# A decode step on one Trainium2 core: PV in four column tiles of N=128, one PSUM group and one scaling per batch, all batches in one loop

## The chip, the core and the metric

The kernel runs on one NeuronCore of a Trainium2 chip. The core has five engines that run on their own and meet at semaphores: TensorE (PE in the profile; its weight loads are PEld), VectorE (DVE), ScalarE (ACT), GpSimd (POOL) and SyncE (SP), which here does nothing but issue DMAs. SBUF and PSUM have 128 partitions[...]. The metric is device microseconds of one execution. Before the change the median of five runs is 193.3 us (193.22 to 193.56).

## The reference, cut to what matters

One decode token for each of 8 batches: attention over the last 2048 positions of a cache of 8192, with 32 query heads on 8 KV heads of 128, then an output projection and an MLP.

```python
W = min(4096, max(256, Sk // 4))                       # 2048
rep = Hq // Hkv                                        # 4
x = A_x
q = (layernorm(x) @ wq).reshape(B, 1, 32, 128).transpose(0, 2, 1, 3)
k = jnp.repeat(k_cache[:, :, Sk - W:, :], rep, axis=1)
v = jnp.repeat(v_cache[:, :, Sk - W:, :], rep, axis=1)
p = softmax(einsum("bhqd,bhkd->bhqk", q, k) * Dh ** -0.5)
o = einsum("bhqk,bhkd->bhqd", p, v)
h = x + o.transpose(0, 2, 1, 3).reshape(B, 1, 4096) @ wo
x = layernorm(h)
h2 = gelu(layernorm(x) @ w3) @ w4                      # hs is zero for one token
out = h + x + h2
```

The inputs are bf16. B_w1 and B_w2 have no influence on the result for a sequence of one token, and the kernel doesn't load them.

## The kernel before, in words

**Tiles.** K and V of a batch are each two tiles of four KV heads (`gq` 0 and 1), 2048 KB per tile: 16 K tiles and 16 V tiles. A tile lies in one of ten SBUF slots (`slots`, 16 KB per partition): partition p holds 64 positions of one of its four heads. The last two slots hold `wq` first and `wo` at the end; `w3` and `w4` take K slots at the end.

**Loads.** SP issues everything on one queue in the order of the list `order` (L229): wq, four K tiles, two V tiles at once; then, alternating, a K tile four ahead and a V tile, each after a wait until the slot's earlier user is done (`free_slot`, L253: `sem_Thi` for K, `sem_PV` for V); then the last V tiles, wo in four pieces, w3 in two, w4 in three.

**One K tile** is worked on in four quarters (t = 0 to 3 for the first tile of a batch, 4 to 7 for the second). `pe_T` (L456) turns a quarter into 16 transposes of 128x128 into one of two PSUM tiles `kT_ps`. ScalarE takes out the first half (`act_Elo`, L494), VectorE the second (`dve_Ehi`, L498), into `kT_sb`. `pe_QK` (L502) then multiplies: four matmuls of N=512 in four column tiles of 32, one for each KV head, all 64 of a batch into one bank of `S_ps`. A quarter can be transposed once the quarter two before it has been taken out.

**Softmax** of a batch: VectorE finds the maximum (`dve_max`), ScalarE makes the exponentials in two halves (`act_exp`), TensorE transposes them (`pe_P`, L480, 16 transposes, into the same `kT_ps`), VectorE multiplies by a 0/1 mask that keeps each head's own rows (`dve_pT`, L572), which gives the weights `pT_sb` for PV. The sums take a fp32 matmul (`pe_LB`), a reciprocal and a product (`dve_rL`).

**PV** of a V tile (`pe_PV`, L581) is 16 matmuls with 64 columns of weights and N=512: the moving side is four position quarters times 128, so each of the four query positions in PSUM has its result in another quarter of the bank. VectorE gathers them with one scaled copy and three scaled adds (`dve_O1`, L602), TensorE adds partitions with `hsel` (`pe_oT`), VectorE copies to `o_all` (`dve_oT`). At the very end `pe_place` and the copies behind it spread `o_all` over 128 partitions as `opl`, for the projection (`pe_proj`).

**Order.** Batch 0 is written out; batches 1 to 7 are a loop on TensorE (`pe_block`, L663, `pe_main`, L701). A pass with batch i transposes and scores batch i, makes P of batch i-1 and PV of batch i-2, so that PV and other work lie between steps that wait. The parts with PV stand in branches that the first pass leaves out (`If_ne`, L667). VectorE and ScalarE have no loop: their instructions are listed in order (L716 and following). Where TensorE waits in the loop, it uses `need`: an instruction that waits for a semaphore and subtracts what it waited for.

**Tail.** After the loop come PV of the last two batches, placement, the projection (128 matmuls, each group of wo pieces behind its wait), statistics, w3 (56 matmuls), gelu, and w4 (56 matmuls of N=128 in four column tiles, behind waits for three pieces), then the store.

Of the kernel before, what the change touches and what calls it, by code (L numbers as in the profile page):

```python
# [11 lines left out]
B = 8  # L12
# [19 lines left out]
NS = 10  # L32
# [4 lines left out]
def bass_sequential_preLN__sliding_block_cached__mixer_s_mlp__decode_kernel(  # L37
# [24 lines left out]
    with es:  # L62
# [30 lines left out]
        P_sb = sb([128, CC * 128], dt.bfloat16, "P_sb")  # L93
        pT_sb = sb([128, 2, CC, 64], dt.bfloat16, "pT_sb")
        maskT = sb([128, CC // 2 * GL, 32], dt.bfloat16, "maskT")
        sel = sb([128, GL], dt.float32, "sel")
        headc = sb([128, NT * R], dt.float32, "headc")
        lspread = sb([128, 128], dt.float32, "lspread")
        par_sel = sb([128, 2, GL * R], dt.float32, "par_sel")
        hsel = sb([128, GL * R], dt.float32, "hsel")  # L100
        gq_of = sb([128, 2], dt.float32, "gq_of")
        qi_of = sb([128, NT], dt.float32, "qi_of")
        mrl = sb([128, 2, 2, NT], dt.float32, "mrl")
        o_sum = sb([128, 2, DH], dt.float32, "o_sum")
        mtile = sb([128, 3, 32], dt.float32, "mtile")
        mrow = sb([128, 3, 32], dt.float32, "mrow")
        lcol = sb([128, 2, 2], dt.float32, "lcol")
        lsum = sb([128, 1], dt.float32, "lsum")
        lsel = sb([128, 2], dt.float32, "lsel")
        rL = sb([128, 2, 2], dt.float32, "rL")  # L110
        iota_f = sb([128, 128], dt.float32, "iota_f")
        selp = sb([GL * R, NT, 4 * GL * R], dt.bfloat16, "selp")
        o_all = sb([GL * R, 2, B, DH], dt.bfloat16, "o_all")
# [28 lines left out]
        pv_ps = [misc, b6]  # L142
        LB = S_ps[:, 1, 0:2]
        OT = slice(0, DH)
        H3 = slice(384, 384 + FC * B)

        sem_slot = [S(f"sem_slot{i}") for i in range(NS)]
# [20 lines left out]
        sem_lsel = S("sem_lsel")  # L168
        sem_LB = S("sem_LB")
        sem_qc = S("sem_qc")  # L170
        sem_PV = S("sem_PV")
        sem_O1 = S("sem_O1")
        sem_oTm = S("sem_oTm")
        sem_oT = S("sem_oT")
        sem_oTA = S("sem_oTA")
        sem_pl = S("sem_pl")
# [31 lines left out]
        POOL_ZERO = 3  # L208

        def pool_prog(e):  # L210
            e.memset(eps_t[:, 0:1], EPS)
            e.memset(eps_t[:, 1:2], EPS * EPS / (1.0 + EPS))
            e.memset(zrow_b[:], 0.0)
            e.memset(scratch[:], 1.0).then_inc(sem_pool, 1)
            e.iota(iota_f[:], [[1, 128]], base=0, channel_multiplier=-1,
                   allow_small_or_imprecise_dtypes=True).then_inc(sem_pool, 1)
            e.memset(mean_w[:], 1.0 / D)
            e.memset(qcur[:], 0.0)
            e.memset(mtile[:], 0.0)
            e.memset(mrow[:], 0.0)  # L220
            e.memset(selp[:], 0.0).then_inc(sem_pool, 1)
# [6 lines left out]
        early = NTILE - 2  # L228
        order = [("k", t) for t in range(4)] + [("v", 0), ("v", 1), ("k", 4), ("v", early), ("k", 5)]  # L229
        for t in range(2, NTILE - 4):  # L230
            order += [("v", t), ("k", t + 4)]
        order += [("v", t) for t in range(NTILE - 4, NTILE) if t != early]
        order += [("wo", 0), ("wo", 1), ("w3", 0), ("w4", 0)]
        place = {("wo", 0): NS - 2, ("wo", 1): NS - 1, ("w3", 0): 0, ("w4", 0): 1}
        for t in range(NTILE):
            place["k", t] = 4 + t if t < 2 else t % 2
            place["v", t] = 4 + t - (NTILE - 4) if t >= NTILE - 4 else 2 + t % 2
        use = {}
        for key in order:
            use[key] = 1 + sum(place[k] == place[key] for k in use)  # L240
        for t in (-2, -1):
            place["v", t] = 4 + t
            use["v", t] = 0
# [6 lines left out]
        def sp_prog(e):  # L250
            e.dma_start(wq_sb, A_wq.rearrange("(p k) n -> p (k n)", k=KC)).then_inc(sem_wq, 16)

            def free_slot(kind, t):  # L253
                if kind == "k" and t >= 4:
                    e.wait_ge(sem_Thi, NT * (t - 1))
                elif kind == "v" and NTILE - 4 <= t < NTILE - 2:
                    e.wait_ge(sem_Thi, NT * (t - (NTILE - 4) + 1))
                elif kind == "v" and 2 <= t < NTILE - 4:
                    e.wait_ge(sem_PV, t - 1)
                elif kind == "wo":  # L260
                    e.wait_ge(sem_peP, PEP_Q2)
                elif kind in ("w3", "w4"):
                    e.wait_ge(sem_Thi, NITEM if kind == "w4" else NITEM - NT)

            for kind, t in order:
                free_slot(kind, t)
                slot = place[kind, t]
                dst = slots[:, slot, :]
                if kind in "kv":
                    b, gq = divmod(t, 2)  # L270
                    cache = A_k_cache if kind == "k" else A_v_cache
                    src = cache[b, GL * gq:GL * (gq + 1), W0:SK, :].rearrange("g (p c) d -> p g (c d)", c=C)
                    e.dma_start(dst, src).then_inc(sem_slot[slot], 16)
                elif kind == "wo":
# [11 lines left out]
                else:  # L286
                    w4_rows = B_w4.rearrange("(c p j) n -> p c (j n)", p=128, j=2)
# [20 lines left out]
        def dve_ident(e):  # L308
# [5 lines left out]
            with nc.allow_low_precision("sums of one 1 and zeros"):  # L314
                ins = e.tensor_reduce(sel[:, 0:GL], ident_f[:, :].rearrange("p (a g) -> p g a", g=GL), AX.X, ALU.add)
            chain(e, ins, "dve_self", dve_self)
            ins = e.tensor_copy(maskT[:, :, :].rearrange("p (c g) x -> p c g x", g=GL),
                                bass.AP(tensor=sel[:, :].tensor, offset=0, ap=[[GL, 128], [0, CC // 2], [1, GL], [0, 32]]))
            chain(e, ins, "dve_self", dve_self)
            with nc.allow_low_precision("sums of one 1 and zeros"):  # L320
                e.tensor_reduce(headc[:, :].rearrange("p (g r) -> p g r", r=R),
                                ident_f[:, :].rearrange("p (g x r) -> p g r x", g=GL, r=R), AX.X, ALU.add)
                e.tensor_reduce(par_sel[:, :, :].rearrange("p a (g r) -> p a g r", r=R),
                                ident_f[:, :].rearrange("p (a g q r) -> p a g r q", a=2, g=GL, r=R), AX.X, ALU.add)
                e.tensor_reduce(gq_of[:, :], ident_f[:, :].rearrange("p (g a x) -> p a g x", g=GL, a=2), AX.XY, ALU.add)
                ins = e.tensor_reduce(qi_of[:, :], ident_f[:, :].rearrange("p (a q r) -> p q a r", q=NT, r=R), AX.XY, ALU.add)
            chain(e, ins, "dve_self", dve_self)
            hc = bass.AP(tensor=headc[:, :].tensor, offset=0, ap=[[NT * R, 128], [R, GL], [0, NT], [1, R]])
            for a in range(2):
                e.tensor_scalar(lspread[:, 64 * a:64 * (a + 1)].rearrange("p (g q r) -> p g q r", g=GL, r=R),  # L330
                                hc, 0.25, None, ALU.mult)
            e.wait_ge(sem_pool, POOL_ZERO)
            for q in range(NT):
                e.tensor_copy(selp[:, q, :].rearrange("p (m q) -> p q m", q=NT)[:, q, :], ident_f[0:GL * R, 0:GL * R])
# [622 lines left out]
```

## Time and profile before

| | |
|---|---|
| median of five runs | 193.3 us (193.22 to 193.56) |
| the profiled execution | 193.35 us; its span, first to last instruction, 191.6 us |
| TensorE busy, weight loads busy | 145.1 us (76%), 98.4 us (51%) |
| VectorE, ScalarE, GpSimd busy | 105.5 us (55%), 90.4 us (47%), 1.9 us (1%) |
| moved by DMA | 79.31 MB, mean 414 GB/s over the span |
| transposes of K (L473) | 1024, 67.8 us busy |
| evictions of K, ScalarE (L496) and VectorE (L500) | 64 each, 1028 and 688 ns |
| QK (L516), PV (L595) | 256 matmuls in 22.5 us, 256 in 31.8 us |
| VectorE gathering PV (L608, L611) | 64 instructions, 22.3 us |
| mean granted TensorE clock | 0.968 |

How to read it: busy time is a union, so engines that work side by side each count in full, and the share says nothing on who waits for whom. In the slices of the page each digit is the busy share in tenths of one fortieth of the span, 4.8 us. A timeline row gives the start, the time, the engine, the line, the operation with what it writes and reads, and the number of instructions run together; in brackets stands how long the engine was idle before and who ended that. "DMA share" of a window is the mean busy share of the 16 DMA engines. The chain of waits is followed back from the last instruction to what released each step.

### The profile page before, as it was taken

Reading aid. Unit: us, or ns where it says so; the run is one execution under the profiler, and the core shown is the slowest. Engines: PE = TensorE matmul, PEld = TensorE weight load, DVE = VectorE, ACT = ScalarE, POOL = GpSimd, SP = SyncE. Lnnn points to the kernel's source line nnn. Section 1 sums busy time; section 2 is a strip of 40 time slices with the busy share of each in tenths; the row PEclk is TensorE's granted clock in tenths of the full one; section 3 lists DMA queues with packets and bytes.
Section 4 is the critical chain, followed back from the end, with each engine's and each line's share of the span. In section 5 each row is a group of like instructions: output and inputs, shape, how many; then the busy total and the mean of one; then the engine's idle time right before and its main releaser. Section 6 shows DMA issues by size and latency. Waiting matters only on the chain. (4 is left out here: it accounts for less than half of the span.)

```text
span 191.6 us, 4850 instructions
## 1 busy us (share of the span) xinstructions
PE 145.1 (76%) x2028; PEld 98.4 (51%) x2028; DVE 105.5 (55%) x287; ACT 90.4 (47%) x113; POOL 1.9 (1%) x14
## 2 busy tenths in 40 slices
PE   2027998797698769886988698958896888776854
PEld 0003976573656455645564557454655465343742
DVE  6401757564647474747474747565665657585141
ACT  3301676862746275526553664347344835406041
POOL 4000000000000000000000000000000000000000
PEclk9999999999999999999999999999999999999755
DMA  6999999999999999999999999999999999999991
GB/s 221 438 421 434 424 424 434 426 434 424 434 424 431 428 438 431 434 431 434 419 431 431 434 431 433 431 434 434 424 424 434 431 434 434 431 438 393 417 403 48
DMA packets 6857, 79.31 MB, mean 414 GB/s; under 512 B 688, under 2 KB 704, under 8 KB 2368
## 3 DMA queue, kind: packets, MB, share of 16 engines
q1 hardware_dynamic: 6832, 79.18, 97.4%
q8 instruction: 6, 0.10, 0.2%
q10 hardware_dynamic: 16, 0.01, 0.0%
q14 instruction: 3, 0.02, 0.0%
HBM read 79.18 MB, written 0.01 MB: 413 GB/s over the span
## 5 line engine op out<-in xcount | busy, mean ns | idle before, releaser
L496 ACT ACTIVATE kT_sb<-kT_ps 128x1024 bf16<-128x1024 bf16 x64 | 64.7, 1028 | 67.3 <-PE kT_ps L473 66.9
L473 PE MATMUL kT_ps<-perm_b,slots 128*128 128x128 bf16 x1024 | 67.8, 222 | 23.7 <-PEq L454 23.5
L473 PEld LDWEIGHTS kT_ps<-perm_b,slots 128*128 128x128 bf16 x1024 | 60.0, 100 | 34.6 <-issue 34.5
L500 DVE COPY kT_sb<-kT_ps 128x1024 bf16<-128x1024 bf16 x64 | 43.5, 688 | 26.2 <-PE kT_ps L473 26.1
L516 PE MATMUL S_ps<-kT_sb,qcur 128*32 128x512 bf16 x256 | 22.5, 387 | 0.8 <-PEq L454 0.8
L546 ACT ACTIVATE P_sb<-S_ps,mtile 128x1024 bf16<-128x1024 f32 x16 | 17.8, 1115 | 2.6 <-DVE mtile L537 2.5
L595 PE MATMUL b<-slots,pT_sb 128*64 128x512 bf16 x128 | 16.5, 384 | 1.2 <-PEq L454 1.2
L577 DVE TENSOR_TENSOR pT_sb<-kT_ps,maskT 128x1024 bf16<-128x1024 bf16 x16 | 10.5, 686 | 10.7 <-PE kT_ps L489 10.7
L595 PE MATMUL misc<-slots,pT_sb 128*64 128x512 bf16 x128 | 15.3, 382 | 0.6 <-PEq L454 0.6
L526 DVE TENSOR_REDUCE mtile<-S_ps 128x1 f32<-128x512 f32 x8 | 5.5, 692 | 13.6 <-PE S_ps L516 13.6
L595 PEld LDWEIGHTS misc<-slots,pT_sb 128*64 128x64 bf16 x128 | 6.7, 109 | 8.4 <-issue 3.6
L595 PEld LDWEIGHTS b<-slots,pT_sb 128*64 128x64 bf16 x128 | 6.2, 109 | 9.2 <-issue 5.7
L516 PEld LDWEIGHTS S_ps<-kT_sb,qcur 128*32 128x32 bf16 x256 | 5.3, 93 | 8.3 <-issue 4.2
L489 PEld LDWEIGHTS kT_ps<-ident_b,P_sb 128*128 128x128 bf16 x128 | 7.2, 98 | 4.1 <-issue 4.1
L489 PE MATMUL kT_ps<-ident_b,P_sb 128*128 128x128 bf16 x128 | 8.7, 219 | 0.6 <-PEq L454 0.6
L611 DVE SCALAR_TENSOR_TENSOR o_sum<-b,mrl,o_sum 128x128 f32<-128x128 f32 x24 | 8.4, 351 | 0.8
L611 DVE SCALAR_TENSOR_TENSOR o_sum<-misc,mrl,o_sum 128x128 f32<-128x128 f32 x24 | 8.4, 351 | 0.8
L395 PE MATMUL S_ps<-slots,xlnT 128*8 128x512 bf16 x32 | 3.6, 626 | 5.7 <-DMA slots<-in_A_wq_dram 5.7
L626 DVE CAST o_all<-misc 16x128 bf16<-16x128 f32 x7 | 1.9, 279 | 7.0 <-PE misc L620 7.0
L412 DVE TENSOR_SCALAR q_sb<-S_ps 128x512 bf16<-128x512 f32 x1 | 0.7, 691 | 9.1 <-PE S_ps L395 9.1
L395 PEld LDWEIGHTS S_ps<-slots,xlnT 128*8 128x8 bf16 x32 | 1.0, 117 | 7.5 <-issue 7.5
L657 ACT ACTIVATE opl<-kT_ps 128x224 bf16<-128x224 f32 x1 | 1.2, 1181 | 6.6 <-PE kT_ps L649 6.6
(104 smaller groups left out, 82.3 us busy)
## 6 DMA issues: line engine op xcount, KB each, us to landing
slots<-in_A_k_cache_dram SPq DMA_DIRECT2D x16, 2048.0 KB, 14.2
slots<-in_A_v_cache_dram SPq DMA_DIRECT2D x16, 2048.0 KB, 16.6
slots<-in_A_wq_dram SPq DMA_DIRECT2D x1, 4096.0 KB, 12.3
slots<-in_A_wo_dram SPq DMA_DIRECT2D x1, 2048.0 KB, 30.7
slots<-in_B_w_dram SPq DMA_DIRECT2D x2, 896.0 KB, 32.0
slots<-in_A_wo_dram SPq DMA_DIRECT2D x1, 1024.0 KB, 32.5
slots<-in_A_wo_dram SPq DMA_DIRECT2D x2, 512.0 KB, 33.7
slots<-in_B_w_dram SPq DMA_DIRECT2D x1, 1024.0 KB, 25.7
```

Source lines behind the costliest of these rows:

```text
L395: ins = e.matmul(S_ps[32 * j:32 * j + B, k, :], xlnT[:, kc * B:(kc + 1) * B], wq_v[:, kc, n0:n0 + 512], start=(kc == 0), stop=(kc == KC - ...
L473: ins = e.matmul(kT_ps[t % 2][:, c * 128:(c + 1) * 128], src[:, c * 128:(c + 1) * 128], perm_b[:, :], is_transpose=True)
L489: ins = e.matmul(kT_ps[half][:, c * 128:(c + 1) * 128], P_sb[:, half * W // 2 + c * 128:half * W // 2 + (c + 1) * 128], ident_b[:, :], is_ ...
L496: e.activation(kT_sb[:, i % NKT, 0:W // 2], kT_ps[i % 2][:, 0:W // 2], ACT.Copy).then_inc(sem_Elo, 1)
L500: e.tensor_copy(kT_sb[:, i % NKT, W // 2:W], kT_ps[i % 2][:, W // 2:W]).then_inc(sem_Ehi, 1)
L516: ins = e.matmul(S_ps[32 * gl:32 * (gl + 1), 0, :], qcur[:, GL * gq + gl, o:o + 32], kv[:, gl, :, :], start=(t == 0), stop=(t == 2 * NT - ...
L526: ins = e.tensor_reduce(mtile[:, 2, 0:1], S_ps[:, 0, :], AX.X, ALU.max)
L546: e.activation(P_sb[:, half * W // 2:(half + 1) * W // 2].rearrange("r (k g) -> r k g", g=GL), s_rep, ACT.Exp, bias=mtile[:, j, 0:1], scal ...
L577: e.tensor_tensor(pT_sb[:, :, half * hc:(half + 1) * hc, :].rearrange("p a c (g x) -> p (c g) a x", g=GL), kT_ps[half][:, 0:W // 2].rearra ...
L595: ins = e.matmul(pv_ps[gq][64 * a:64 * (a + 1), :].rearrange("p (q d) -> p q d", d=DH), pT_sb[:, gq, cc, :], vq[:, cc, :, :], start=(cc < ...
L611: ins = e.scalar_tensor_tensor(o_sum[:, gq, :], pv_ps[gq][:, q * DH:(q + 1) * DH], w[:, q:q + 1], o_sum[:, gq, :], ALU.mult, ALU.add)
L626: e.tensor_copy(o_all[:, gq, b, :], pv_ps[gq][0:GL * R, OT]).then_inc(sem_oT, 1)
```

## The change

- **PV** takes one V row of 128 per matmul: 64 matmuls of N=128 per V tile, with 32 columns of weights, in four column tiles of 32, one for each quarter q of the positions. Both V tiles of a batch add into one PSUM group (`pv_ps`, 128x128): the weights of a tile are 32 columns of a row of 48 in `pT_sb` whose other half is zero, so that heads of the one tile add nothing to the other.
- **Scaling**: one VectorE multiply by `rL` per batch (`dve_O1`) takes the place of two times four. The sums come straight from the two columns `lsum` that the exponentials leave, by two fp32 matmuls (`pe_LB`); the additions and products around them go.
- **Placement**: per batch four fp32 matmuls with `selw` (`pe_OP`) add the partitions and spread the result, and ScalarE copies it to `opl` (`act_OP`). `hsel`, `o_all`, `pe_oT`, `dve_oT`, `pe_place` and their copies go.
- **Loop**: all eight batches run in one loop on TensorE. A pass does the first four transposes, P and sums of the batch before, QK and the other transposes, the last QK, then PV and placement of the batch before, in a branch that the first pass leaves out. PV is one batch late, not two. The q transposes stand before the loop and so before the first K transposes. The loop's head is put at the start of an instruction block.
- **Loads**: nine slots. K tiles alternate between two slots, V tiles between two, the last batch's V tiles and w3 have slots of their own. SP's order is K0, K1, the last batch's first V tile, K2, V0, K3, V1, then per batch two K and two V tiles. K tile t waits until K tile t-2 is transposed; V tiles wait for the half of PV that used their slot.
- GpSimd clears `selw`, `lsum`, `P_sb` and `pT_sb` at the start; the constants of VectorE change with the layout.

```diff
-NS = 10
+NS = 9
-        pv_ps = [misc, b6]
-        LB = S_ps[:, 1, 0:2]
+        pv_ps = misc[:, 0:DH]
+        LB = S_ps[:, 1, 0:1]
...
+        order = [("k", 0), ("k", 1), ("vl", 0), ("k", 2), ("v", 0), ("k", 3), ("v", 1)]
+        for b in range(1, NB - 1):
+            order += [("k", 2 * b + 2), ("k", 2 * b + 3), ("v", 2 * b), ("v", 2 * b + 1)]
+        order += [("vl", 1), ("wo", 0), ("wo", 1), ("w3", 0), ("w4", 0)]
...
+                    if kind == "k" and b:
+                        e.wait_ge(sem_Thi, NT * (t - 1))
+                    if kind == "v" and b:
+                        e.wait_ge(sem_PV[gq], b)
...
+        def pe_P(e, i, half):
+            need(e, sem_exp, 2 * i + half + 1)
+            n = min(2 * NT * i + 3 + half, 2 * NT * NB)
+            need(e, sem_Elo, n)
+            need(e, sem_Ehi, n)
...
+        def pe_LB(e):
+            if e is not None:
+                for half in range(2):
+                    ins = e.matmul(LB, lspread[:, :, :].rearrange("p q h -> p (q h)"), lsum[:, half:half + 1],
+                                   start=(half == 0), stop=(half == 1))
+                ins.then_inc(sem_LB, 1)
...
+        def pe_PV(e, slot, gq, cs=range(CT)):
+            for c in cs:
+                for q in range(NT):
+                    k = q * CT + c
+                    ins = e.matmul(pv_ps[32 * q:32 * (q + 1), :], pT_sb[:, c, q, 16 * gq:16 * gq + 32],
+                                   slots[:, slot, k * DH:(k + 1) * DH], start=(gq == 0 and c == 0),
+                                   stop=(gq == 1 and c == CT - 1), tile_position=(0, 32 * q), skip_group_check=True)
+            if c == CT - 1:
+                ins.then_inc(sem_PV[gq], 1)
+
+        def dve_O1(e, b):
+            e.wait_ge(dve_self, cnt["dve_self"])
+            e.wait_ge(sem_PV[1], b + 1)
+            e.tensor_scalar(o_sum[:, :], pv_ps, rL[:, :], None, ALU.mult).then_inc(sem_O1, 1)
...
+        def pe_OP(e, b):
+            need(e, sem_O1, b + 1)
+            if e is None:
+                return
+            for q in range(4):
+                ins = e.matmul(op_ps(b), selw[:, q, :], o_sum[:, NJ * q:NJ * (q + 1)], start=(q == 0), stop=(q == 3))
+            ins.then_inc(sem_OP, 1)
...
+        def pe_block(e, i, later=None):
+            p = 2 * NT * i
+            for t in range(NT):
+                pe_T(e, i, t)
+            pe_P(e, i, 0)
+            pe_P(e, i, 1)
+            pe_LB(e)
+            pe_QK(e, p)
+            pe_QK(e, p + 1)
+            for t in range(NT, 2 * NT):
+                pe_T(e, i, t)
+                pe_QK(e, p + t - 2)
+            pe_QK(e, p + 6)
+            pe_QK(e, p + 7)
+            if i == 0:
+                return
+            with nullcontext() if e is None else e.If_ne(later, 0):
+                log.append("later")
+                for gq in range(2):
+                    need(e, sem_v[gq], 16 * i)
+                    if e is not None:
+                        pe_PV(e, 2 + gq, gq)
+                pe_OP(e, i - 1)
...
+            with nc.Fori(0, NB, engines=(mybir.EngineType.PE,), head_slot={mybir.EngineType.PE: 0}):
+                pe_block(e, 1, later_on)
+                e.reg_mov(later_on, 1)
...
+        def pe_last(e):
+            pe_P(e, NB, 0)
+            pe_P(e, NB, 1)
+            pe_LB(e)
+            e.wait_ge(sem_vl[0], 16)
+            for half in range(2):
+                need(e, sem_pT, 2 * NB + 1 + half)
+                pe_PV(e, 4, 0, range(half * CT // 2, (half + 1) * CT // 2))
+            e.wait_ge(sem_vl[1], 16)
+            pe_PV(e, 5, 1)
+            pe_OP(e, NB - 1)
```

On ScalarE a batch is now its eight evictions, the two exponentials, and the copy of the placement of the batch before; on VectorE the eight evictions with the two mask products and the reciprocal of the batch before after the fourth, then maximum, `dve_qc` for the next batch and `dve_O1` of the batch before.

## The prediction

> **What bounds the kernel now.** I read the slices of the page first, then the DMA queues, then the chain of waits, then twenty-microsecond windows.
>
> ```profile
> DMA  6999999999999999999999999999999999999991
> ...
> q1 hardware_dynamic: 6832, 79.18, 97.4%
> ```
>
> The sixteen DMA engines are busy from the second slice to the last but one, and one queue fills 97.4% of their span. The reader is to see that there is no hole anywhere.
>
> ```profile
> 161.04 5.46 SPq L291
> ...
> 166.55 21.53 DMA slots<-in_B_w_dram
> ...
> 188.12 0.60 PE b L887 x8
> ```
>
> This is the chain that ended last: the w4 transfer, issued long before, lands at 188.08, and what follows it (sixteen and eight matmuls, the casts, the store) takes 3.5 us to the end of the span. No wait on compute stands in it.
>
> ```profile
> 100.00:120.00 20.00, 16.56 (x228) 11.22 (x225) 12.31 (x34) 10.49 (x13) 0.00 (x0) 1.00 1.01 431
> ```
>
> In the middle the queue moves 431 GB/s at a DMA share of 1.01. A K or V tile has 2048 KB = 2.097 MB, so it takes 2.097/431 = 4.87 us, and the four tiles of a batch 19.46 us; in the timeline the same eight score matmuls recur at 82.82 and 102.27, 19.45 apart. The batch period is the DMA's. TensorE stood 1.85 us before the first transpose of that batch (87.16) waiting for K. So the old kernel has about 1.8 us of spare TensorE time per batch, and in the tail the final matmuls start at 186.91, only 1.2 us ahead of the landing that decides.
>
> The bytes do not change. The new kernel can be faster only if the DMA itself runs fuller, and is slower once (a) TensorE's batch is longer than about 19.3 us, (b) a transfer is issued after its turn has come, or (c) the tail arrives later than w4.
>
> **(a) TensorE's batch, part by part.** The new loop is serial: eight K transposes (T), the softmax transposes (P), eight score steps (QK), PV and placement (OP) of the batch before, with no work kept back to fill waits. The rows used are from the timeline (start, duration, engine, line, count, and in brackets the idle time before):
>
> ```profile
> 82.82 0.61 PE L516 MATMUL S_ps<-kT_sb,qcur 128*32 128x512 bf16 x8
> ...
> 83.36 1.92 PE L595 MATMUL misc<-slots,pT_sb 128*64 128x512 bf16 x16
> ...
> 87.16 1.80 PEld L473 LDWEIGHTS kT_ps<-perm_b,slots 128*128 128x128 bf16 x32 [1.85 <-issue]
> ...
> 89.13 0.91 PEld L473 LDWEIGHTS kT_ps<-perm_b,slots 128*128 128x128 bf16 x16 [0.17 <-issue]
> ...
> 99.47 1.07 PE L473 MATMUL kT_ps<-perm_b,slots 128*128 128x128 bf16 x16
> ```
>
> Sixteen transposes take 0.91 us of issue; two T run back to back and the third starts 1.97 after the first, because the evictions of the first must be done. Four QK matmuls cost 0.21 (eight in 0.61, four in 0.40). A semaphore wait costs about 0.1 when it is met, 0.17 to 0.2 from a late eviction to the next load.
>
> From the first T at 0: T3 starts at 2.9; its DVE eviction ends at 2.9 + 1.05 + 0.04 + 0.69 = 4.7; the second half of P starts at 4.85 and takes 0.46; two fp32 matmuls for the sums (four passes; two took 0.30) 0.4: 5.7. Two QK with a wait, 0.53: 6.25. Four times T + QK + wait, 0.91 + 0.21 + 0.1: 11.1. The last QK waits for T7's eviction (T7 at 10.0, so 10.0 + 1.78 + 0.17): 12.0. QK and the branch, 0.1 + 0.42 (82.82 to 83.36 is the same passage): 12.5.
>
> PV: 128 matmuls of 32 columns by 128, not in the trace. Nearest rows:
>
> ```profile
> 178.14 3.49 PE L796 MATMUL S_ps<-opl,slots 128*128 128x8 bf16 x128
> ...
> 186.91 1.02 PE L887 MATMUL b<-slots,gT 128*8 128x128 bf16 x32 [0.59 <-DMA slots<-in_B_w_dram]
> ```
>
> L887 has N=128 in four column tiles too, each with a new load: (1.02 - 0.31)/31 = 23 ns each, at half clock. L796 shows what a pair of load and matmul costs when little streams: (3.49 - 0.17)/127 = 26 ns. I take 25 ns: 3.2 us per batch, where the old PV took 2 x 1.92 = 3.8. Ends: 22 ns, and 57 ns (a transpose[...]): 2.8 and 7.3 us.
>
> [...] The old PV row[...]: (1.92 - 0.38)/15 = 103 ns per matmul in two column tiles is half of 0.21, so its 64-column loads were hidden. [...]
>
> After PV: last matmul out 0.25, DVE scale 0.05 + 0.345 (L608), wake 0.17, OP four fp32 matmuls (eight passes at about 0.11): 0.9 to 1.2, branch and loop end 0.4 to 0.5. Sum: 12.5 + 3.2 + 0.8 + 1.1 + 0.5 = 18.1; with the second V tile of the batch before, due at 14.6 (three tiles after K), PV's second half starts 0.6 later. I take **18.5 us**, against 19.46: 0.9 us spare, half of what there was. That also holds the O1 wait: the next batch's transposes are queued behind OP on TensorE, and on ScalarE the first eviction behind OP's copy; both are inside the 18.5.
>
> Costed at nothing: max and exp (1.65 + 2.3 us) lie beside PV and are done at 16.2, before P wants them; in the second iteration no PV covers them, and ScalarE's first eviction queues behind exp, some 3 us once, absorbed by the 8 us of queued transfers below. DVE loses seven of eight o_sum steps per batch (2.9 to 0.35 us), but nobody waited long for it. The mask product keeps 1024 elements with runs of 16 as before (0.69); were it 1.2, T5 would still not wait. POOL's new memsets (5120 elements at 480 per 0.49 us) end near 8 us; first use is after 20. The loop's code: the old run fetches six blocks of 16 KB (q8, at 24, 33, 45, 175, 182 and 187 us), so none once the loop has gone round twice; the new body is half as long again and spans three such blocks, as many as the old one touches, so I cost its back edge at nothing too (at the back edge near 82.9 the eight QK loads of both sides run without a gap). If a block had to be fetched again on every pass, at 0.9 us or more each, this would be the first rival below.
>
> **(b) SP's order.** Two K slots instead of four early ones. Within a batch K(2i+2) is released by T3 (4.0) and its turn is at 14.6; K(2i+3) by T7 (11.1) for 19.5; the V tiles by PV's halves (14.2, 16.6) for 24.3 and 29.2. The least lead is 8.4 us; an issue needs about 1.2 (first issue 0.73, and the 431 GB/s line meets zero at 1.9). Only the start is close: the third K tile waits for the first to be transposed, which now stands behind the q transposes. q is ready at 17.53; eight transposes at half clock (0.107) to 18.44; T0 and T1 likewise to 21.9, T2 and T3 at about 22 to 23.9, as the old clock rose near 22.2; release 24.1, first byte 25.3. The one-microsecond windows add up to 10.5 MB (wq, K0, K1, one V) at 26.8. Spare 1.5 us; 0.1 if the clock stays low.
>
> **(c) Tail.** After the last K tile three V tiles (14.6 us), wo, w3 and w4 follow, as before. The loop's passes start at 18.4, 33.5 (K2's landing) and 55.2 (33.5 + 18.5 + the 3 us above), then gain 0.9 each on the data until they wait for K again, near 110. The last pass starts with K14 at about 150.1 and ends at 168.7; P, sums, mask 2.5, PV 3.2, scale and OP 1.6: projection ready near 176, before 177.96. Its last quarter waits for wo (issued 145.8, 33.7 to landing: 179.5), ends near 180.2 against 181.6, so the final matmuls could start near 185.5. They still end on w4 at 188.08 and 188.7. Gain on the path: nothing.
>
> Sum against the profiled execution (193.35 = 191.6 span + 1.75 around it, 0.05 over the median of the five): 0. **Forecast 193.3 us.**
>
> **Rivals.**
> - *TensorE becomes the bound (slower, 0.27).* Place: PV in the loop. It decides from a batch of about 19.3 us (55.2 + 0.8 + 6 x 19.3 = 171.8, against 168.7 and a tail slack of 2 to 3), that is 31 ns per PV matmul, or 0.8 us of branches and fp32 passes that I missed; every further 0.1 costs about 0.6. [...] At 19.6: about +2, 195. For it: all waits are now in series. Against it: the 23 and 26 ns rows.
> - *The third K tile is late (slower, 0.08).* A hole of up to 1 us near 27 that nothing later fills: **193.9**.
> - *The DMA's straggler changes (faster, 0.19).* The last bytes trickle (158 GB/s from 187, 10 GB/s from 188), so one engine ends late. Instruction fetches are 0.2% of 16 x 191.6 = 6.1 engine-us over six packets, 1.0 us each on one engine. Another spread of them takes off up to 1.0: **192.7**. Against it: nearly the same number of TensorE instructions.
> - *No change (0.46):* 193.0 to 193.7.
>
> About 0.2% (0.4 us) is what a measurement can tell from no change. Faster 0.19, same 0.46, slower 0.27 + 0.08 = 0.35. The range runs from 192.6, the straggler's gain, to 198, which takes in a batch of up to 20 us[...].
>
> **What would show it.** PV groups of 64 matmuls in 1.4 to 1.9 us; a pause of TensorE before the first T of each batch, waiting for K; DMA slices 9 throughout; projection near 176 to 178; the chain ending in w4. Wrong if TensorE goes from OP straight into T0 in every batch, if the DMA slices show holes, or if the chain ends in compute.

## The result: 194.46 us, 0.5% slower

| | before | after |
|---|---|---|
| median | 193.35 us (48 runs, 193.08 to 193.74) | 194.46 us (28 runs, 193.27 to 196.49) |
| ratio | 1 | 1.0052, 95% interval 1.004 to 1.0064 |
| the profiled execution, its span | 193.35, 191.6 us | 195.52, 193.7 us |
| mean granted TensorE clock | 0.968 | 0.885 |

The ratio leaves out two of the 28 runs (196.38 and 196.49), which count as slow because they are over 1.5% above the fastest; the median of the other 26 is 194.41. The changed kernel's best runs are level with the old kernel; what is new is a spread of 2.5 us even without those two. The time lies inside the forecast's range, but the forecast was "no change".

The page of the changed kernel, slices and DMA queue:

```profile
PEclk9999999589999975999999957996999799997555
DMA  6999999999999999999999999999999999999980
GB/s 225 433 430 430 426 430 426 426 433 433 396 387 433 433 428 433 430 433 426 433 430 433 433 430 433 430 433 433 433 426 430 430 433 433 433 413 410 412 336 9
...
q1 hardware_dynamic: 6832, 79.18, 96.5%
```

The DMA digits still read 9 from the second slice to the 38th; in the middle only the GB/s row has two low slices, 396 and 387 (48 to 58 us), and the queue's share fell from 97.4 to 96.5%. The clock row has low slices in the loop (5 to 8, where the old row reads 9 up to its last three slices).

The chain of waits ends as before, in w4 and two groups of matmuls:

```profile
164.23 2.98 SPq L269
...
167.25 22.99 DMA slots<-in_B_w_dram
...
190.29 0.60 PE b L761 x16
```

So the end is still set by the DMA: w4's second piece lands at 190.24, against 188.08. The trace has sixteen completions for each transfer, one for each DMA engine; the first of them shows when an engine is free for the next transfer, and the last shows when the tile is complete. By these, two terms make the 2.2 us between the two profiled executions. The DMA engine that is first to finish w4's last piece does so at 187.31 instead of 186.81 (+0.50: something was lost earlier, for all engines). The last one lags 3.55 us behind it instead of 1.91 (+1.64).

**Where the first term arose.** Two-microsecond windows of the changed kernel; the last two columns are the DMA share and GB/s:

```profile
48.00:50.00 2.00, 1.64 (x28) 1.01 (x26) 1.02 (x2) 1.24 (x2) 0.00 (x0) 1.00 0.99 426
50.00:52.00 2.00, 2.00 (x132) 1.82 (x128) 1.56 (x6) 0.04 (x1) 0.00 (x0) 1.00 1.00 401
52.00:54.00 2.00, 1.38 (x24) 1.32 (x17) 0.35 (x1) 2.00 (x3) 0.00 (x0) 1.00 0.94 369
54.00:56.00 2.00, 1.93 (x35) 1.79 (x33) 1.10 (x2) 2.00 (x5) 0.00 (x0) 1.00 0.93 360
```

The same stretch of the kernel before, whose rows scatter around 431:

```profile
52.00:54.00 2.00, 1.66 (x26) 1.16 (x28) 1.59 (x4) 2.00 (x5) 0.00 (x0) 1.00 1.05 451
54.00:56.00 2.00, 2.00 (x18) 0.71 (x16) 0.40 (x2) 0.97 (x2) 0.00 (x0) 1.00 0.97 418
```

Against 431 GB/s the changed kernel's windows from 50 to 56 lack 30, 62 and 71 GB/s for 2 us each: 0.33 MB, or 0.76 us. This is the sixth K tile (K5): on the first engine the tile before it lands at 51.27 and K5 at 56.80, 5.53 us later where 4.86 is the pace. SP's issues (line 247) show why:

```profile
29.61 0.53 SPq L247 DMA_DIRECT2D slots<-in_A_k_cache_dram  x1
...
40.48 9.02 SPq L247 DMA_DIRECT2D slots<-in_A_k_cache_dram  x2
51.24 1.43 SPq L247 DMA_DIRECT2D slots<-in_A_v_cache_dram  x2
```

The two issues in the second row are K4 (40.48) and K5: 40.48 + 9.02 - 0.53 = 48.97. K5's turn comes when the first engine has finished K4, at 51.27. It is issued 2.3 us ahead of its turn (this is its lead), the transfers around it about 5 us or more. The old kernel issued its K5 at 43.81 for a turn at 51.43, a lead of 7.6:

```profile
43.81 0.54 SPq L273 DMA_DIRECT2D slots<-in_A_k_cache_dram  x1
```

And TensorE (transposes of the second pass of the changed kernel) shows what K5's release waited for:

```profile
33.94 6.51 PE L440 MATMUL kT_ps<-perm_b,slots 128*128 128x128 bf16 x64 [3.06 <-PEq L423]
...
43.89 1.05 PE L440 MATMUL kT_ps<-perm_b,slots 128*128 128x128 bf16 x16 [0.99 <-PEq L423]
...
47.86 1.07 PE L440 MATMUL kT_ps<-perm_b,slots 128*128 128x128 bf16 x16
```

K5 takes K3's slot, which is free after the second pass's last four transposes. They cannot start before K3 is complete: on the first engine it lands at 41.55, on the last at 43.60. They run from 43.89 to 48.9. By the trace, most of this lag of 2.05 us came with a code fetch: the last completion was 0.64 us behind the first on K0 and 1.96 on K1, and between them lies a fetch of 16 KB for TensorE (21.00 us, 0.88 us long). In the old kernel the lag grew in the same way, from 0.61 us on K1 to 1.70 on K2, with the fetch at 24.49. No run took that fetch away. Also seen: the first four quarters' transposes take 6.5 us instead of 4.0, at half clock (granted 0.50 from 33.0 to 39.8 us) after a pause of 3.06 us, but they are done before K3 is there.

**PV itself** was no burden. Weight loads in the middle of the span:

```profile
105.60 0.93 PEld L537 LDWEIGHTS misc<-slots,pT_sb 128*32 128x32 bf16 x64 [0.15 <-issue]
...
109.32 0.97 PEld L556 LDWEIGHTS b<-o_sum,selw 128*128 128x128 f32 x8 [0.76 <-issue]
112.48 1.63 PEld L440 LDWEIGHTS kT_ps<-perm_b,slots 128*128 128x128 bf16 x16 [2.19 <-issue]
```

Sixty-four of the 128 matmuls take 0.93 us of issue, 14.5 ns each, and TensorE still stands 2.19 us before the next batch's first transpose.

### The profile page after: what moved, and what is told of

Same layout as the page of the kernel before. It is cut to its first block, busy times and chain, and to the rows that moved or that the text cites. A ratio compares the mean times of both kernels' runs of the same rounds, so it can differ in the third digit from the quotient of the medians.

```text
span 193.7 us, 6348 instructions
## 1 busy us (share of the span) xinstructions
PE 145.2 (75%) x2848; PEld 118.2 (61%) x2848; DVE 85.8 (44%) x183; ACT 93.1 (48%) x119; POOL 6.4 (3%) x17
## 3 DMA queue, kind: packets, MB, share of 16 engines
q1 hardware_dynamic: 6832, 79.18, 96.5%
## 5 line engine op out<-in xcount | busy, mean ns | idle before, releaser
L440 PE MATMUL kT_ps<-perm_b,slots 128*128 128x128 bf16 x1024 | 75.2, 238 | 11.9 <-PEq L423 11.7
L440 PEld LDWEIGHTS kT_ps<-perm_b,slots 128*128 128x128 bf16 x1024 | 68.1, 108 | 22.2 <-issue 22.1
L537 PE MATMUL misc<-slots,pT_sb 128*32 128x128 bf16 x1024 | 16.2, 219 | 2.4 <-PEq L423 2.4
L537 PEld LDWEIGHTS misc<-slots,pT_sb 128*32 128x32 bf16 x1024 | 14.7, 97 | 3.9 <-issue 3.8
L527 DVE TENSOR_TENSOR pT_sb<-kT_ps,mask 128x1024 bf16<-128x1024 bf16 x18 | 12.4, 689 | 3.6 <-PE kT_ps L456 3.5
L456 PE MATMUL kT_ps<-perm_p,P_sb 128*128 128x128 bf16 x144 | 10.9, 218 | 3.2 <-PEq L423 3.2
L456 PEld LDWEIGHTS kT_ps<-perm_p,P_sb 128*128 128x128 bf16 x144 | 8.5, 98 | 5.2 <-issue 5.0
L556 PE MATMUL b<-o_sum,selw 128*128 128x32 f32 x56 | 8.1, 292 | 4.3 <-PEq L423 4.3
L556 PEld LDWEIGHTS b<-o_sum,selw 128*128 128x128 f32 x56 | 7.5, 210 | 5.3 <-issue 5.3
L288 DVE TENSOR_SCALAR ident_f<-iota_f 128x128 f32<-128x128 f32 x1 | 5.7, 5685 | 1.3 <-POOL iota_f L207 1.3
```

What stands on the lines that cost most here:

```text
L288: e.tensor_single_scalar(ident_f[:], iota_f[:], 0.0, ALU.is_equal)
L440: ins = e.matmul(kT_ps[t % 2][:, c * 128:(c + 1) * 128], src[:, c * 128:(c + 1) * 128], perm_b[:, :], is_transpose=True)
L456: ins = e.matmul(kT_ps[half][:, c * 128:(c + 1) * 128], P_sb[:, k * 128:(k + 1) * 128], perm_p[:, :], is_transpose=True)
L527: e.tensor_tensor(bass.AP(tensor=pT_sb[:, :, :, :].tensor, offset=h0 * NT * 48, ap=[[CT * NT * 48, 128], [48, CT // 2 * NT], [32, 2], [1, ...
L537: ins = e.matmul(pv_ps[32 * q:32 * (q + 1), :], pT_sb[:, c, q, 16 * gq:16 * gq + 32], slots[:, slot, k * DH:(k + 1) * DH], start=(gq == 0 ...
L556: ins = e.matmul(op_ps(b), selw[:, q, :], o_sum[:, NJ * q:NJ * (q + 1)], start=(q == 0), stop=(q == 3))
```

## The experiments

Theory H: K5 is issued too late for its turn, and the hole is most of the loss. Theory F: TensorE's instruction fetches hold up single DMA engines near the end. Theory C: the half clock after TensorE's pauses makes the work late. The kernel before was timed beside each group (193.31 to 193.40).

**e1_k3first: K3 ahead of V0.**

```diff
-order = [..., ("k", 2), ("v", 0), ("k", 3), ("v", 1)]
+order = [..., ("k", 2), ("k", 3), ("v", 0), ("v", 1)]
```

> The fourth K tile (K3) is put ahead of the first V tile in SP's order; nothing else. Theory H (a hole in the DMA queue at the sixth K tile, K5: it is issued 2.3 us before its turn at 51.27 because the second pass waits for K3, which lands at 43.60 behind V0): K3 lands 4.9 us sooner, the second pass's fifth transpose starts at about 42.9 and not 43.86, K5 is issued at about 48.0, its lead grows to about 3.3 us, K4 to K5 takes 4.9 us and not 5.5, and the time falls by about 0.5 to 0.7 us, to 193.8. But K3's own lead shrinks from 7 to about 2.2 us, so a smaller hole may open at 32 us. Theory F (an instruction fetch of TensorE holds up one DMA engine near the end, about 1.6 us in the profiled run): time and spread as before, 194.4, single times from 193.3 to 196.5. Theory C (TensorE at half clock after its pauses makes the tail late): no change, 194.4.

Measured 194.9 us (ratio 1.0073, 1.0061 to 1.0085), no gain where Theory H had forecast 193.8. The hole moved to K3, as the expectation feared, in the windows of this run:

```profile
30.00:32.00 2.00, 2.00 (x32) 1.15 (x29) 1.12 (x2) 1.69 (x2) 0.00 (x0) 1.00 0.82 344
32.00:34.00 2.00, 0.48 (x8) 0.13 (x4) 1.30 (x4) 0.15 (x1) 0.00 (x0) 1.00 0.76 279
```

K3 was issued at 31.6 for a turn at 32.0 and took 1.47 us over the pace; K5, now with a lead of 4.3, lost nothing (52.95 to 57.82, 4.87 us). The loss went with the lead, not with the tile.

**e2_halves: every odd K tile in two halves.**

```diff
-                        e.wait_ge(sem_Thi, NT * (t - 1))
+                        e.wait_ge(sem_Thi, NT * (t - 1) - 2 * gq)
...
+                    if kind == "k" and gq:
+                        n = C * DH // 2
+                        e.dma_start(slots[:, slot + gq, :n], src[:, :, :n]).then_inc(sem[gq], 16)
+                        if b:
+                            e.wait_ge(sem_Thi, NT * (t - 1))
+                        e.dma_start(slots[:, slot + gq, n:], src[:, :, n:]).then_inc(sem[gq], 16)
...
```

> Each odd K tile is loaded in two halves of 8 KB per partition, the first of which waits only for the first two of the four transposes that free its slot; the order of tiles is unchanged. Theory H: the first half of K5 is issued about 2.7 us sooner, at about 46.3 (lead 5 us), the second at 48.9 (lead 4.8), the hole at 51 to 56 us is gone, K4 to K5 takes 4.9 us, and the time falls by 0.7 us or more, to 193.4 to 193.8, with a narrower spread. Theory F: the hole goes, but most of the loss stays: 194.1 to 194.4, with single times still up to 196. Theory C: no change. If 8 KB pieces are slower in themselves, all K intervals grow and the time goes above 194.5.

Measured 193.82 us (21 runs, 193.54 to 194.91; ratio 1.0027, 1.0018 to 1.0035). K5 took 4.93 us, and 0.64 of the 1.11 us between the medians came back. The first engine ended at 187.26, as late as in the changed kernel, though without this hole. Where that time went is not settled: K2, with a lead of 2.8 us, took 0.12 of it, and if the eight halved tiles took the rest of the 0.45 us against the old kernel, that is 0.04 us each.

**e3_plain and e4_half_plain: the loop's head not aligned,** without and with the halves.

```diff
-nc.Fori(0, NB, engines=..., head_slot={mybir.EngineType.PE: 0})
+nc.Fori(0, NB, engines=...)
```

> The loop's head is no longer aligned (the head slot is left out), so TensorE's code moves by 157 instructions against the fetched blocks; nothing else. Theory F: TensorE's instruction fetches near the end (174.9, 180.9, 187.6 us) move by several us or one goes, another DMA engine ends last, and the time moves by 0.5 us or more, with another spread; a fetch may come into the loop, which would cost more. Theory H: the hole at 51 to 56 us stays, median 194.4, spread as before. Theory C: the same, 194.4.

> Both edits: the odd K tiles in halves, and the loop's head not aligned. Theory H: as with the halves alone, 193.4 to 193.8. Theory F: as with the head not aligned alone. If both hold, their gains add, down to about 193.0. Theory C: 194.4.

194.69 us (193.47 to 196.11; 1.0046 to 1.0092) and 193.89 us (193.69 to 196.42; 1.0027 to 1.0064): each median like that of its aligned twin. But four of e4's 22 runs lie between 195.4 and 196.5, where none of e2's 21 is above 194.91; what these four lost is not shown. In e3 the fetches near the end moved by 0.4, 0.4 and 1.5 us (to 175.3, 181.3, 189.0). Where the code lies was not the matter for the median, as far as this edit moved it.

The profiled execution of e3 (194.52, near the changed kernel's median) says more on the two terms. K5 had a lead of 2.56 us there and took only 0.25 over the pace, and the last engine's lag at the end was 2.67 us, 0.76 over the old kernel's. So the two terms change from run to run, and the hole is not always the larger one.

**e5_k5half and e9_k5half_again: K5 alone in halves.** The second half counts for TensorE; VectorE takes the first half's semaphore before the mask product that TensorE waits for anyway.

```diff
-e.wait_ge(sem_Thi, NT * (t - 1))
+e.wait_ge(sem_Thi, NT * (t - 1) - 2 * (t == 5))
...
+if (kind, t) == ("k", 5):
+    n = C * DH // 2
+    e.dma_start(slots[:, slot + gq, :n], src[:, :, :n]).then_inc(sem_k5, 16)
+    e.wait_ge(sem_Thi, NT * (t - 1))
+    e.dma_start(slots[:, slot + gq, n:], src[:, :, n:]).then_inc(sem[gq], 16)
...
+if b == 1 and half == 0:          # dve_pT
+    e.wait_ge(sem_k5, 16)
```

> Only the sixth K tile (K5) is loaded in two halves, the first of them after two of the four transposes that free its slot; all other tiles in one piece. Theory H (the late K5 is most of the loss): no hole at 51 to 56 us, and without the small cost of the other tiles' half pieces (the first DMA engine was 0.45 us later at the end in the run with all odd K tiles halved, 0.02 to 0.03 per tile), the most frequent time is 193.3 to 193.5, the median 193.5, with single runs up to 194.9 from an engine that an instruction fetch held up. Theory F (fetches, not the hole): median 194.0 or more. Theory C (half clock): 194.4.

> The kernel with K5 alone in halves once more, for a narrower comparison and as the base of this group. Theory H: 193.4 as measured, level with the kernel before (ratio 1.000 to 1.001), single runs up to 194.9 at most. Theory F: with more runs the spread of the changed kernel (193.3 to 196.5) comes back, median above 193.8.

193.41 us (5 runs, ratio 1.001, 0.9998 to 1.0022) and 193.47 us (13 runs, 193.23 to 194.08; 1.0013, 1.0005 to 1.0022). SP's issues of the two halves in e5_k5half:

```profile
46.23 0.54 SPq L250 DMA_DIRECT2D slots<-in_A_k_cache_dram  x1
48.89 0.53 SPq L252 DMA_DIRECT2D slots<-in_A_k_cache_dram  x1
```

The second half goes out when the whole tile went out before, but its turn is now half a tile later. The windows of e5_k5half:

```profile
52.00:54.00 2.00, 1.38 (x21) 1.39 (x18) 0.35 (x1) 2.00 (x4) 0.00 (x0) 1.00 0.98 414
54.00:56.00 2.00, 1.94 (x36) 1.79 (x34) 1.17 (x2) 2.00 (x5) 0.00 (x0) 1.00 1.04 438
```

K5 lands 4.91 us after K4. Of the 1.11 us between the medians some 1.0 is back, and the 13 runs of e9 spread over 0.9 us. Changing when one of the 32 tile loads is issued takes away nearly all of the loss; 0.1 us remains.

**e7_warm: no pause after the first pass.**

```diff
+with e.If_eq(later, 0):
+    for _ in range(24):
+        e.matmul(S_ps[:, 1, 256:512], perm_b[:, :], kT_sb[:, 0, 0:256], start=True, stop=True)
```

> The changed kernel with 24 idle matmuls of N=256 (into a part of a PSUM bank that nobody reads) after the first pass of the loop only, so that TensorE isn't idle between 30.6 and 33.9 us. Theory H with the wait where the trace has it: the second pass's first four transposes run at full clock, 2.5 us shorter, but its fifth still waits for K3 at 43.6, K5 is still issued at about 48.9, the hole stays: 194.4. Theory C: K5 is issued at about 46.5, the hole goes and the time falls to 193.5.

195.26 us (1.0064 to 1.0126): slower, which neither theory had. TensorE of this run:

```profile
30.63 2.79 PE L580 MATMUL S_ps<-kT_sb,perm_b 128*128 128x256 bf16 x24
...
43.58 1.87 PE L440 MATMUL kT_ps<-perm_b,slots 128*128 128x128 bf16 x16 [3.23 <-PEq L423]
...
45.93 1.89 PE L440 MATMUL kT_ps<-perm_b,slots 128*128 128x128 bf16 x16
```

The transposes of the pass's first four quarters ran at full clock (1.95 us for two quarters) and were done sooner; TensorE then stood 3.2 us waiting for K3, and the half clock fell on three of the last four, which take 1.8 to 1.9 us instead of 1.05 (the granted clock reads 0.54 from 48 to 50 us). That moved K5's issue from 48.97 to 51.43:

```profile
37.92 14.04 SPq L247 DMA_DIRECT2D slots<-in_A_k_cache_dram  x2
```

K5 then took 6.92 us, 2.06 over the pace, and the time is 1.95 over that of the kernel before. So theory C holds in one form: the clock matters where it delays the release of that slot, here by 2.5 us. It may be a source of the changed kernel's spread; its slower runs were not profiled, so that is not shown.

**e11_k5half_warm: both.** The edits of e5 and e7.

> K5 alone in halves, and the idle matmuls after the first pass, which move TensorE's half clock from the second pass's first four transposes to its last four (43.6 to 51). Theory H (only the issue of K5 against its turn counts): the halves are issued at about 48.3 and 51.4 for turns at 51.3 and 53.8, a lead of 3.0 and 2.4: loss 0 to 0.6 us, 193.4 to 194.0, where the same fillers with K5 in one piece gave 195.3. Theory C (the half clock itself): as there, 195.

193.92 us (12 runs, 193.26 to 195.70; ratio 1.0028, 1.0014 to 1.0042), against 195.26 with the tile in one piece. The half clock is there in the profiled executions of both (0.54 in e7's window; in e11 the two halves go out 3.57 us apart, in e5 2.66); what differs is when K5 is issued. The profiled execution (195.70, the slowest) had the second half issued at 51.66 with a lead of 2.0 us, where the forecast had 2.4 and a loss of at most 0.6; K5 and the V tile behind it, whose lead was 2.3, took 11.83 us instead of 9.72, a loss of 2.1.

**e10_before_k5_late: the same fault put into the old kernel.**

```diff
-e.wait_ge(sem_Thi, NT * (t - 1))
+e.wait_ge(sem_Thi, NT * (t - 1) + 2 * (t == 5))
```

> The kernel before, with one wait made longer: its sixth K tile, issued at 43.8 us for a turn at 51.4, now also waits for the first two of the four transposes of the fifth tile, at about 50.2; nothing else is late. Theory H: a hole of (50.2 + 2.1 - 51.4) = 0.9 us there, which nothing fills: 194.1 to 194.4, as much as the change itself costs. If transfers that are queued elsewhere or later slack absorb a single late tile: 193.3.

195.87 us (ratio 1.0126, 1.0104 to 1.0148), 2.5 us more than the kernel before. The issue, then the windows:

```profile
52.15 0.54 SPq L273 DMA_DIRECT2D slots<-in_A_k_cache_dram  x1
```

```profile
50.00:52.00 2.00, 2.00 (x21) 2.00 (x20) 0.69 (x1) 2.00 (x4) 0.00 (x0) 0.50 0.63 270
52.00:54.00 2.00, 2.00 (x22) 2.00 (x20) 1.73 (x5) 2.00 (x4) 0.00 (x0) 0.50 0.48 147
```

It was meant to go out at 50.2, but TensorE was at half clock here too (the 0.50 in both rows, with a pause of 3.4 us before) and it went at 52.15, for a turn at 51.42. The tile took 7.56 us, 2.70 over the pace. The forecast of 194.1 to 194.4 was for an issue at 50.2, without the half clock. Little of it was given back later: the first engine ends w4 2.69 us after that of the kernel before (189.50 against 186.81), and only the last engine caught up in the hole (its lag fell from 1.83 to 0.58 us and was 1.68 at the end, against 1.91).

**The price of a late issue,** from the first engine's landings:

| run, late tile | issued, us | turn (landing of the tile before), us | issue + 2.0 - turn, us | tile's interval, over 4.86 us | median over that of before, us |
|---|---|---|---|---|---|
| after, K5 | 48.97 | 51.27 | below 0 | 0.67 | 1.11 |
| e1, K3 | 31.57 | 32.02 | 1.55 | 1.47 | 1.5 |
| e7, K5 | 51.43 | 51.44 | 1.99 | 2.06 | 1.95 |
| e10, K5 | 52.15 | 51.42 | 2.73 | 2.70 | 2.51 |

The 2.0 us come from the last two rows and fit e1. Three tiles of e6 (below) fit as well: with leads of 1.04, 0.27 and -0.18 us they took 1.09, 1.77 and 2.14 over the pace, where the sum gives 0.96, 1.73 and 2.18. The packets show of what the 2.0 us consist: the first data packet starts 1.34 (e7) and 1.40 us (e10) after the issue, and as all sixteen engines start again within half a microsecond, their first packets take 0.6 to 1.2 us, most of them about 1, instead of 0.61.

By this sum the changed kernel's profiled run should just have made it. It did not: 13 to 15 of 16 engines were busy from 51.25 to 52.0, and packets were slow until 56 (the longest 2.38 us). Nor does the sum cover e11's profiled run. The traces of all runs show how wide the uncertain zone is: of the K and V tiles in one piece, those with leads of 2.3 to 3.6 us took between nothing and 0.67 over the pace (and 1.66 the V tile in e11), and none with a longer lead took more than 0.1. The third K tile was at that edge too: in e1, e2 and e5 its lead was 2.8 to 3.4 us, and it took 0.12 to 0.34 over. Why a lead of over 2 us can still lose time was not settled. In other runs the half clock may reach the last four quarters, as in e7, and the loss grow to 2 us.

**e8_pv_twice: PV doubled,** on e5. The loop does each PV group a first time into a PSUM region that nobody reads.

```diff
+e.matmul(S_ps[32 * q:32 * (q + 1), 1, 256:384], pT_sb[:, c, q, 16 * gq:16 * gq + 32], ...)
 pe_PV(e, 2 + gq, gq)
```

> As the run with K5 alone in halves, and the loop does the PV matmuls of each batch twice, the first time into a PSUM region that nobody reads. The trace of the changed kernel has PV at 1.97 us per batch and TensorE waiting 1.7 to 2.2 us for K before each batch's first transpose. If that spare time is real, 2 us more fits almost exactly: 193.5, at most 195 (0.2 us over the pace in each of six batches). If TensorE were already the bound, it costs 2 us in each of seven batches: above 205.

195.1 us (194.12 to 196.12; ratio 1.0057 to 1.0126). In the profiled execution (194.12) TensorE goes from the placement straight to the next batch:

```profile
91.21 1.05 PE L565 MATMUL b<-o_sum,selw 128*128 128x32 f32 x8 [0.62 <-PEq L430]
92.33 3.96 PE L447 MATMUL kT_ps<-perm_b,slots 128*128 128x128 bf16 x64
```

There is no wait for K left, and yet w4's last piece lands first at 186.90, no later than in e5 (187.05). So about 2 us per batch were spare, and with them gone TensorE is just at the bound: the other three runs are 0.5 to 2 us slower, past the forecast of 193.5 and at most 195. They were not profiled, so what they lost is not shown.

**e6_pool_code: fourteen more code fetches,** on e5: GpSimd executes 1792 one-byte memsets from 50 us on.

```diff
+e.wait_ge(sem_Thi, 4 * NT)
+for n in range(1792):
+    e.memset(spare[0:1, n:n + 1], 0)
```

> As the run with K5 alone in halves, and GpSimd executes 1792 one-byte memsets that nobody waits for, from about 49 us on: seven more blocks of 16 KB of code to fetch, while the data is exactly the same. Theory F': each fetch holds up one of the sixteen DMA engines by about 1 us, and as they are never idle the lag stays to the end; with seven more fetches on engines that are not spread evenly, the last engine ends 0.5 to 2 us later: median 194.0 to 195.5. If fetches cost the end nothing (they are only 0.06 us of sixteen engines each): as the other run, 193.5.

201.78 us (ratio 1.0441, 1.0424 to 1.0459), far more than expected. The queue row of the page, 17 packets instead of 3 in the changed kernel, and a window:

```profile
q14 instruction: 17, 0.14, 0.2%
```

```profile
100.00:112.00 12.00, 11.27 (x207) 8.86 (x209) 6.79 (x11) 6.23 (x7) 10.34 (x311) 0.94 0.92 375
```

The code came in 14 pieces of 8 KB, not in 7 of 16, about one every 4.9 us, 0.31 us each. The last DMA engine's lag behind the first grew from 1.8 us (tile at 61 us) to 7.8 (105 us), while the last but one stayed at 1.8 and the median engine at 0.4: these fetches hit one and the same engine. A tile is complete with its last engine, so the slots came free later and holes opened for all (375 GB/s). For theory F this shows that a few fetches on one engine can move the end by as much as the profiled execution's 1.64 us; that TensorE's fetch at 187.56 did so there is read from the trace alone: it falls between the landings of the other fifteen engines (186.67 to 188.59) and that of the last, 190.24. In the profiled executions of e1 to e5, e7, e8, e9 and e11 the lag at the end was 1.8 to 2.7 us, so the 3.55 of the changed kernel's is the exception.

So the cause of most of the loss in the median is shown by what was changed: e5 and e9 moved K5's issue alone, left six fetches of 16 KB for TensorE as before, and 1.0 of 1.11 us went; e10 put a late K5 into the old kernel and lost 2.5. What is not shown is the size of K5's hole in the changed kernel's other runs. The holes in the two profiled executions with K5 in one piece and nothing else of the loads changed (0.67 in the changed kernel, 0.25 in e3) are smaller than that 1.0 us.

## Why the prediction was wrong, step by step

- **What bounds the kernel:** right. The end is w4's landing in both kernels, and what was lost was lost in the DMA queue.
- **(a) TensorE's batch, 18.5 us with PV at 25 ns per matmul:** safe by too much. PV took 14 to 15 ns (0.93 us for 64), 1.97 us per batch and not 3.2, and the pause for K was about 2 us, not 0.9. The row that was taken as nearest, the w4 matmuls at 23 ns, stood at half clock (granted 0.50), and the sum used it unconverted; at full clock it says 12 (an estimate: half of 23). Most of the row at 26 ns lies there too (from 179.48). TensorE as the bound, the likeliest way to be slower at 0.27, needed 31 ns per matmul and fell with the 14.5; e8 shows that it decides about 2 us of work per batch later.
- **(b) SP's order: the step that failed.** "The least lead is 8.4 us" was worked out for a batch in the steady state, where the K tiles of a pass are there before its transposes want them, and the start was examined for the third K tile only (in the profiled execution that one was in time, issued at 22.14 for a turn at 26.96). The second pass was passed over with "absorbed by the 8 us of queued transfers". But there K3 itself has just landed. Between K3 and K5 in the queue stand V1 and K4, 9.7 us. K3 is complete 2.05 us after the first engine has finished it, since the last engine decides; the four transposes and scores take 5.3; that leaves 2.3 us. Both were to be had: the old trace's engines end a tile 1.6 to 2.0 us apart from the third K tile on, and the prediction itself priced four T with QK and waits at 4.9. Its 1.2 us from issue to the first bytes was nearly right (1.34 and 1.40), but a queue that has run dry loses more than that: 2.0. The 8.4 us did not hold in the steady state either: after K5, the second K tile of each batch was issued 3.3 to 6.3 us ahead of its turn, since a pass begins with the last engine's landing, not the first's, and some passes ran in part at half clock. These leads sufficed, with intervals of 4.86 and 4.87 us.
- **The clock** was assumed full in the loop, and weighed for the first pass only; this belongs to the same step. In the changed kernel's profiled execution the granted clock was 0.50 in five stretches of the loop. The first (33 to 40 us) came with a pause of 3.1 us and cost nothing at K5; the other four began near pauses of 0.6 to 2.1 us, while the old kernel's pause of 1.9 us (before 48.37) left the clock full. In e7 and e10 it halved within pauses of 3.2 and 3.4 us, and there it delayed K5's issue. So the clock halved near pauses of 0.6 to 3.4 us and stayed full after one of 1.9; what decides among these was not settled.
- **(c) The tail:** right. The projection starts at 175.59 (forecast 176), its last quarter waits for wo, and the final matmuls wait for w4.
- **The code's cost in the loop, nothing:** right for the loop itself; no fetch of a 16 KB code block falls between 36 and 174 us. But most of the lag that left K5 so late came with the fetch at 21.00, before K3.
- **The DMA's straggler, as a gain of up to 1.0:** only a gain was priced. In the profiled execution the lag lost 1.64.
- **The forecast:** 193.3 where 194.46 came. The mechanism of the rival "third K tile late" (a hole of up to 1 us that nothing fills, 193.9) was the right one, at the wrong tile. That K2 itself was in time in the profiled execution was in part luck: its margin was as thin as the prediction said in other runs (leads of 2.8 to 3.4 us).

## What to carry to other kernels

When buffers are cut, work out the lead of every transfer in the first two rounds, not in the steady state alone: its turn by the fastest DMA engine, and its release by the slowest one's landing of the tile that it replaces. Here a lead under 2 us lost the difference, one of 2.3 to 3.6 us could lose time, and a longer one cost at most 0.1. A queue that was full to the end gave back little of what one late issue cost, and a tile split in two by release order mended it without another buffer. A row taken from a stage at another clock must be converted before it prices anything.

## What the runs showed of the hardware that was not expected

- A column-tiled matmul of K=128, 32 columns, N=128 with a new load each took 14 to 15 ns here at full clock (0.93 us for 64), about a quarter of the 53 ns (0.21 us for four) that a QK matmul of N=512 took.
- Each of GpSimd's 8 KB fetches in e6 put the same DMA engine back by more than its packet's 0.31 us: from 90 to 105 us, with one fetch in each tile's time, the lag grew by 0.63 to 0.65 us per tile. TensorE's fetches did not all fall on one engine: in the changed kernel, after those at 21.00, 28.68 and 35.08, one, two and then three completions of a tile came 1.8 to 2.1 us behind the first, where all had been within 0.65.
- The last engine's lag stayed while the queue was full (2.0 to 2.1 us from 27 to 186 us in the changed kernel), and went when it ran dry: at the late K5 it fell from 1.53 to 0.62 us in e7 and from 1.83 to 0.58 in e10.
- Two VectorE operations at the start took as long as GpSimd needed to clear its tiles. Rows of VectorE in the changed kernel; in the old one, whose GpSimd was busy for 1.9 us and not 6.4, the same two took 0.87 and 0.79 us:

```profile
1.33 5.68 DVE L288 TENSOR_SCALAR ident_f<-iota_f 128x128 f32<-128x128 f32 x1 [1.33 <-POOL iota_f L207]
1.47 5.61 DVE L289 TENSOR_SCALAR ident_b<-iota_f 128x128 bf16<-128x128 f32 x1
```

They end at 7.01 and 7.08, just after GpSimd's last memset (4.27 + 2.65 = 6.92). Why they took so long is not shown: no run here took the memsets away. It cost nothing: the normalised input was ready at 10.9 us instead of 7.1, and the q matmuls wait for wq until 13.1.
